# Attention followed by a three-way maxout FFN: the attention products regrouped, transposes moved to the DMA engines, and a new order of work

## The chip, the cores and the metric

The kernel runs on one core of one Trainium2 chip. The metric is the device time of one execution in microseconds (us); the kernel before takes 380.43 us as the median of 3 runs (380.34 to 380.91). The engines are called by the profile's names: PE is TensorE's matrix product and PEld its load of the stationary operand (the weights), DVE is VectorE, ACT is ScalarE, POOL is GpSimd, SP is SyncE. A matrix product streams the columns of its moving operand past a stationary operand of at most 128 rows by 128 columns and leaves float32 sums in PSUM, which has 8 banks of 512 float32 per partition.

## The reference, cut to what matters

```python
batch, n_heads, seq, head_dim = (8, 12, 448, 64)          # q, k, v: float32
n_tokens, d_model, d_ff = (3584, 768, 768)

def _attn_ref(q, k, v):
    scale = 1.0 / np.sqrt(q.shape[-1])
    scores = scale * np.matmul(q, k.transpose(0, 1, 3, 2))
    m = np.max(scores, axis=-1, keepdims=True)
    e = np.exp(scores - m)
    attn = e / (np.sum(e, axis=-1, keepdims=True) + np.exp(-m) + 1e-09)
    return np.matmul(attn, v)

def _moe_ref(x, w1, w2, w3, w_out):
    h = np.maximum(np.maximum(x @ w1, x @ w2), x @ w3)
    return h @ w_out

# x: the attention's output as (batch * seq, n_heads * head_dim)
```

Multiplying numerator and denominator by exp(m) gives exp(s) / (sum of exp(s) + 1), so both kernels take exp of the scaled scores without a maximum and add one to the sum.

## The kernel before

The 96 pairs of batch and head are worked in 24 groups of four heads, three groups to a batch. The 448 keys of a head lie in four chunks of 112. The loop interleaves the attention of a group with "pieces" of the FFN of an earlier batch: an up piece is six products of 448 columns into one bank (one of w1, w2, w3 and 128 of the 768 hidden features), an out piece six products of 384 columns. Parts that nothing below speaks of are cut.

```python
SC = 112; NCH = S // SC; GH = 4
ps1 = tile_pool("ps1", bufs=4, PSUM)      # one bank each: transposes, sums of AV, FFN pieces
ps2 = tile_pool("ps2", bufs=2, PSUM)      # two banks each: scores

def transpose_pair(i, pr):                # two heads: K and Q to [dim, token]
    for n, t16 in enumerate((k16, q16)):
        for c in range(NCH):
            nc.tensor.transpose(out=trT[:, n, ts(c, SC)], in_=t16[:, c, :, :], identity=...)
    nc.vector.tensor_copy(out=qkT, in_=trT...)

def scores_visit(i, pr, cs):              # two chunks of 112 keys for two heads
    for c in cs:
        for hh in range(2):
            nc.tensor.matmul(out=stp[:, hh, 0:S],
                lhsT=qkT[hh * D : hh * D + D, c * SC : c * SC + 128],
                rhs=qkT[hh * D : hh * D + D, S : 2 * S], start=True, stop=True)
    for c, stp in zip(cs, stps):
        nc.scalar.activation(out=eT[:, 2*pr : 2*pr+2, c, :], in_=stp[0:SC, :, 0:S],
                             func=AF.Exp, scale=scale)

def av_group(i):                          # sums over the keys, four heads side by side
    def col_tiled(weights):
        for c in range(NCH):
            for hh in range(GH):
                nc.tensor.matmul(out=bank[32*hh : 32*hh+32, 0:S], lhsT=weights(hh, c),
                                 rhs=eT[:, hh, c, :], ...)
    den = col_tiled(ones)                                   # sum of exp
    nc.scalar.activation(out=lnd, in_=den, func=AF.Ln, bias=one_b)
    nc.scalar.activation(out=rb, in_=lnd, func=AF.Exp, bias=ln_lam, scale=-1.0)
    for hf in range(2):
        num = col_tiled(v[:, hh, c, hf::2])                 # half of the 64 dims
        nc.vector.tensor_tensor(out=xT[...], in0=num, in1=rb, op=ALU.mult)

def up_piece(b, fc, i):
    for dc in range(NDC):                                   # 6
        nc.tensor.matmul(out=p_i[:, 0:S], lhsT=w_sb[i][:, dc, ts(fc, 128)],
                         rhs=xT[b][:, dc, :], ...)
    # DVE: copy (i == 0) or maximum with what is in hT

def out_piece(bp, t, nh):
    for fc in range(NFC):                                   # 6
        nc.tensor.matmul(out=op_ps[:, 0:384], lhsT=hT[bp][:, fc, ts(t, 128)],
                         rhs=wout_sb[:, fc, ts(nh, 384)], ...)
    # DVE: times 1/LAMBDA into o_sb; every second piece SP stores 128 rows

for i in range(24):                        # four visits for each group
    for vi, (pr, cs) in enumerate(visits):
        scores_visit(i, pr, cs)
        # vi == 0: FFN pieces, av_group(i - 1), FFN pieces, copies of K and Q by DVE
        # vi == 1, 2: FFN pieces, transpose_pair(i + 1, vi - 1), FFN pieces
        # vi == 3: FFN pieces
av_group(23); add_pieces(7); moe(all)
```

Of the kernel before, what the change touches and what calls it, by code (L numbers as in the profile page):

```python
# [14 lines left out]
ts = bass.ts  # L15

MMDT = FP16
LAMBDA = 256.0


@with_exitstack
def kernel(
# [16 lines left out]
    SC = 112  # L39
    NCH = S // SC  # L40
    NDC = DM // 128
    NFC = DFF // 128
    GH = 4
    NG = H // GH
    scale = 1.0 / math.sqrt(D)

    tabs = list(get_activation_tables(nc.m.arch).keys())
# [10 lines left out]
    cpool = ctx.enter_context(tc.tile_pool(name="const", bufs=1))  # L58
    ld_pool = ctx.enter_context(tc.tile_pool(name="ld", bufs=5))
    p16_pool = ctx.enter_context(tc.tile_pool(name="p16", bufs=2))  # L60
    att_pool = ctx.enter_context(tc.tile_pool(name="att", bufs=4))
    e_pool = ctx.enter_context(tc.tile_pool(name="e", bufs=2))
    small = ctx.enter_context(tc.tile_pool(name="small", bufs=2))
    xt_pool = ctx.enter_context(tc.tile_pool(name="xt", bufs=2))
    ht_pool = ctx.enter_context(tc.tile_pool(name="ht", bufs=2))
    out_pool = ctx.enter_context(tc.tile_pool(name="outp", bufs=3))

    ps1 = ctx.enter_context(tc.tile_pool(name="ps1", bufs=4, space=bass.MemoryType.PSUM))
    ps2 = ctx.enter_context(tc.tile_pool(name="ps2", bufs=2, space=bass.MemoryType.PSUM))

    ctx.enter_context(tc.manual_schedule())

    groups = [(b, g) for b in range(B) for g in range(NG)]
    raw = {}

    def load_group(i, which="qkv", step=GH):
        b, g = groups[i]
        tiles = raw.setdefault(i, {})
        for name in which:
            tiles[name] = ld_pool.tile(  # L80
                [SC, GH, NCH, D], MMDT, tag="ld_" + name, name="ld_" + name
            )
        for h0 in range(0, GH, step):
            for name in which:
                src = {"q": q, "k": k, "v": v}[name][b].rearrange(
                    "(g h) (p c) d -> g p h (c d)", g=NG, c=NCH
                )[g]
                nc.gpsimd.dma_start(  # L88
                    out=tiles[name][:, h0 : h0 + step].rearrange("p h c d -> p h (c d)"),
                    in_=src[:, h0 : h0 + step],  # L90
                )

    load_group(0, "qk", 2)
    ident16 = cpool.tile([128, 128], MMDT, name="ident16")
    make_identity(nc, ident16)
    load_group(1, "qk")
    load_group(0, "v")
    load_group(1, "v")
    load_group(2)
    ones16 = cpool.tile([SC, 32], MMDT, name="ones16")  # L100
    nc.vector.memset(ones16, 1.0)
    one_b = cpool.tile([128, 1], FP32, name="one_b")
    nc.vector.memset(one_b, 1.0)

    ln_lam = cpool.tile([128, 1], FP32, name="ln_lam")
    nc.vector.memset(ln_lam, math.log(LAMBDA))

    w_sb = [cpool.tile([128, NDC, DFF], MMDT, name=f"w{i}") for i in range(4)]
    wout_sb = w_sb[3]

    def load_weight(i):
        w = (moe_w1, moe_w2, moe_w3, moe_w_out)[i]
        for g in range(NG):
            if i < 3:
                src = w.rearrange("(g p hf) f -> g p hf f", g=NG, hf=2)[g]
            else:
                src = w.rearrange("(g hf p) f -> g p hf f", g=NG, hf=2)[g]
            nc.gpsimd.dma_start(out=w_sb[i][:, 2 * g : 2 * g + 2, :], in_=src)


    state = {}

    def pair_qk(i):
        qf, kf = raw[i].pop("q"), raw[i].pop("k")
        qk16 = []
        for pr in range(GH // 2):
            q16 = p16_pool.tile([SC, NCH, 2, D], MMDT, tag=f"q16_{pr}", name=f"q16_{pr}")
            k16 = p16_pool.tile([SC, NCH, 2, D], MMDT, tag=f"k16_{pr}", name=f"k16_{pr}")
            nc.vector.tensor_copy(
                out=k16, in_=kf[:, 2 * pr : 2 * pr + 2].rearrange("p h c d -> p c h d")  # L130
            )
            nc.vector.tensor_copy(
                out=q16, in_=qf[:, 2 * pr : 2 * pr + 2].rearrange("p h c d -> p c h d")
            )
            qk16.append((q16, k16))
        state[i] = {"qk16": qk16, "qkT": []}

    def transpose_pair(i, pr):
        st = state[i]
        q16, k16 = st["qk16"][pr]  # L140
        trT = ps1.tile([128, 2, S], MMDT, tag="bank1", name="trT")
        for n, t16 in enumerate((k16, q16)):
            for c in range(NCH):
                nc.tensor.transpose(  # L144
                    out=trT[:, n, ts(c, SC)], in_=t16[:, c, :, :],
                    identity=ident16[0:SC, 0:SC],
                )
        qkT = att_pool.tile([2 * D, 2 * S], MMDT, tag="qkT", name="qkT")
        nc.vector.tensor_copy(out=qkT, in_=trT.rearrange("p n s -> p (n s)"))  # L149
        st["qkT"].append(qkT)  # L150

    def scores_visit(i, pr, cs):
        st = state[i]
        if "eT" not in st:
            st["eT"] = e_pool.tile([SC, GH, NCH, S], MMDT, tag="eT", name="eT")
        qkT = st["qkT"][pr]
        stps = []
        for c in cs:
            stp = ps2.tile([128, 2, 512], FP32, tag="bank2", name="stp")
            for hh in range(2):  # L160
                nc.tensor.matmul(  # L161
                    out=stp[:, hh, 0:S],
                    lhsT=qkT[hh * D : hh * D + D, c * SC : c * SC + 128],
                    rhs=qkT[hh * D : hh * D + D, S : 2 * S],
                    start=True,
                    stop=True,
                )
            stps.append(stp)
        for c, stp in zip(cs, stps):
            nc.scalar.activation(  # L170
                out=st["eT"][:, 2 * pr : 2 * pr + 2, c, :],
                in_=stp[0:SC, :, 0:S],
                func=AF.Exp,
                scale=scale,
            )

    xT = {}

    def av_group(i):
        b, g = groups[i]  # L180
        st = state.pop(i)
        eT, v16 = st["eT"], raw[i].pop("v")
        if g == 0:
            xT[b] = xt_pool.tile([128, NDC, S], MMDT, tag="xT", name="xT")

        def col_tiled(weights):
            bank = ps1.tile([128, 512], FP32, tag="bank1", name="av")
            for c in range(NCH):
                for hh in range(GH):
                    nc.tensor.matmul(  # L190
                        out=bank[32 * hh : 32 * hh + 32, 0:S],
                        lhsT=weights(hh, c),
                        rhs=eT[:, hh, c, :],
                        start=(c == 0),
                        stop=(c == NCH - 1),
                    )
            return bank

        den = col_tiled(lambda hh, c: ones16[:, :])
        lnd = small.tile([128, S], FP32, tag="lnd", name="lnd")  # L200
        nc.scalar.activation(out=lnd, in_=den[:, 0:S], func=AF.Ln, bias=one_b)  # L201
        rb = small.tile([128, S], FP32, tag="rb", name="rb")
        nc.scalar.activation(out=rb, in_=lnd, func=AF.Exp, bias=ln_lam, scale=-1.0)  # L203
        for hf in range(2):
            num = col_tiled(lambda hh, c: v16[:, hh, c, hf::2])
            nc.vector.tensor_tensor(  # L206
                out=xT[b][:, 2 * g + hf, :], in0=num[:, 0:S], in1=rb, op=ALU.mult
            )

# [4 lines left out]
    def up_piece(b, fc, i):  # L214
        if b % 2 == 0 and fc == 0 and i == 0:
            hT[b // 2] = ht_pool.tile([128, NFC, 2 * S], MMDT, tag="hT", name="hT")
        dst = hT[b // 2][:, fc, (b % 2) * S : (b % 2) * S + S]
        p_i = ps1.tile([128, 512], FP32, tag="bank1", name="p_i")
        for dc in range(NDC):
            nc.tensor.matmul(  # L220
                out=p_i[:, 0:S],
                lhsT=w_sb[i][:, dc, ts(fc, 128)],
                rhs=xT[b][:, dc, :],
                start=(dc == 0),
                stop=(dc == NDC - 1),
            )
        if i == 0:
            nc.vector.tensor_copy(out=dst, in_=p_i[:, 0:S])  # L228
        else:
            nc.vector.tensor_tensor(out=dst, in0=dst, in1=p_i[:, 0:S], op=ALU.max)  # L230

    NH = 2
    NW = DM // NH

    def out_piece(bp, t, nh):
# [45 lines left out]
    def moe(cols):  # L281
# [5 lines left out]
        if not pieces:  # L287
            credit[0] = min(credit[0], 0.0)
# [82 lines left out]
```

## Time and profile before

| What | Value |
|---|---|
| time, median of 3 | 380.43 us |
| span in the profile | 377.6 us |
| PE busy | 358.3 us, 3120 products |
| DVE, ACT, POOL busy | 194.7, 194.5, 59.4 us |
| read from and written to HBM | 42.47 MB, 11.01 MB |
| first FFN product | 39.22 us after the start of the span |
| last FFN product of the last piece | ends at about 373 us |

The profile gives each engine's busy time, the span in 40 slices, the chain of work that ended last, and groups of like instructions with the mean duration of one. Two things are needed to read it. A product's duration (353 ns for 448 columns) is its latency, from the first column in to the last sum out; products in a row overlap, so what a product costs is the distance from its start to the next start. Where the timeline merges a row of x like products that last t us together and d us each, that distance is (t - d) / (x - 1). And the share of a busy engine is an average over a start, a long middle and an end, which have different limits; the stretches of time show them apart.

### The profile page before, as it was taken

To read this page: it belongs to the slowest core of one execution; us is meant where nothing else is said; L and a number is where in the kernel's file an instruction comes from. 1 tells how busy PE (TensorE), PEld (TensorE's weight loads), DVE (VectorE), ACT (ScalarE), POOL (GpSimd) and SP (SyncE) were. 2 spreads that over 40 slices of the span, in tenths; PEclk is the share of its full clock that TensorE was granted. 3 is DMA by queue.
4 is the path that set the end of the run, shared out by engine and by line. 5 is a ranking of instruction groups with operands and counts; after the bars stand their busy time and mean duration, and the time that the engine had idled before them with its cause. 6 is when DMAs were issued, how large, how long until landed. Compare 5 with 4: busy or idle time off the path is not lost.

```text
span 377.6 us, 7320 instructions
## 1 busy us (share of the span) xinstructions
PE 358.3 (95%) x3120; PEld 172.0 (46%) x3120; DVE 194.7 (52%) x395; ACT 194.5 (52%) x241; POOL 59.4 (16%) x92
## 2 busy tenths in 40 slices
PE   2777999999999999999999999999999999999995
PEld 1233444544445444454445544454444554445552
DVE  2233545545546546546546555455465465445553
ACT  1879464663655655555555645546555554552000
POOL 8533450220210201202202202202000000000000
PEclk9999999999999999999999999999999999999999
DMA  7999998555508625455236555077010410013005
GB/s 92 185 208 206 204 196 121 73 136 68 73 2 151 111 54 75 60 139 75 32 43 89 126 101 73 6 128 141 2 26 0 128 43 0 2 32 95 2 0 168
DMA packets 40064, 32.71 MB, mean 87 GB/s; under 512 B 2272, under 2 KB 35296, under 8 KB 40032
## 3 DMA queue, kind: packets, MB, share of 16 engines
q0 software_dynamic: 35552, 21.24, 40.8%
q1 hardware_dynamic: 4480, 11.01, 9.8%
q8 instruction: 24, 0.39, 0.5%
q14 instruction: 8, 0.07, 0.0%
HBM read 42.47 MB, written 11.01 MB: 142 GB/s over the span
## 4 chain that ended last, share of the span: by engine, by line
PE 84%; DMA 9%; ACT 2%; POOL 2%; DVE 1%; issue 1%; DVEq 0%; POOLq 0%
PE p_i L220 43%; PE op_ps L241 15%; PE av L190 11%; PE stp L161 10%; PE trT L144 4%; DMA w_123<-in_moe_w_dram 3%; DMA ld_k<-in_k_dram 3%; DMA ld_q<-in_q_dram 2%; DVE xT L206 1%; ACT eT L170 1%; ACT rb L203 1%; ACT lnd L201 1%; POOL ld_q L88 1%; POOL ld_k L88 1%; POOL ld_v L88 0%
## 5 line engine op out<-in xcount | busy, mean ns | idle before, releaser
L170 ACT ACTIVATE eT<-stp 112x896 f16<-112x896 f32 x192 | 164.9, 916 | 145.1 <-PE stp L161 145.1
L230 DVE TENSOR_TENSOR hT<-hT,p_i 128x448 f16<-128x448 f16 x96 | 59.4, 619 | 45.5 <-PE p_i L220 45.1
L206 DVE TENSOR_TENSOR xT<-av,rb 128x448 f16<-128x448 f32 x48 | 27.8, 619 | 70.8 <-ACT rb L203 64.7
L220 PE MATMUL p_i<-xT,w_122 128*128 128x448 f16 x288 | 63.0, 353 | 0.4
L220 PE MATMUL p_i<-xT,w_123 128*128 128x448 f16 x288 | 62.4, 353 | 0.0
L220 PE MATMUL p_i<-xT,w_124 128*128 128x448 f16 x288 | 62.2, 353 | 0.0
L161 PE MATMUL stp<-qkT 64*128 64x448 f16 x384 | 56.3, 364 | 4.9 <-ACT eT L170 4.8
L241 PE MATMUL op_ps<-w_125,hT 128*128 128x384 f16 x336 | 59.5, 326 | 0.0
L88 POOL DMA_DIRECT2D ld_v<-in_v_dram x24 | 16.8, 702 | 192.3 <-PE av L190 126.3
L248 DVE TENSOR_SCALAR o_sb<-op_ps 128x384 f32<-128x384 f32 x56 | 31.2, 557 | 28.5 <-PE op_ps L241 28.4
L241 PEld LDWEIGHTS <-hT 128*128 128x128 f16 x336 | 30.9, 98 | 24.8 <-issue 6.3
L190 PE MATMUL av<-eT,ld_v 112*32 112x448 f16 x768 | 41.8, 361 | 0.0
L228 DVE CAST hT<-p_i 128x448 f16<-128x448 f32 x48 | 29.7, 620 | 19.9 <-PE p_i L220 19.9
L220 PEld LDWEIGHTS <-w_123 128*128 128x128 f16 x288 | 25.9, 98 | 29.6 <-issue 9.2
L220 PEld LDWEIGHTS <-w_124 128*128 128x128 f16 x288 | 26.0, 98 | 28.7 <-issue 7.8
L220 PEld LDWEIGHTS <-w_122 128*128 128x128 f16 x288 | 26.1, 98 | 27.8 <-issue 7.0
L149 DVE COPY qkT<-trT 128x896 f16<-128x896 f16 x48 | 29.5, 615 | 3.1 <-PE trT L144 3.0
L161 PEld LDWEIGHTS <-qkT 64*128 64x128 f16 x384 | 12.0, 94 | 40.9 <-issue 40.3
L190 PEld LDWEIGHTS <-ld_v 112*32 112x32 f16 x768 | 21.0, 99 | 16.8 <-issue 1.7
L190 PE MATMUL av<-eT,ones_116 112*32 112x448 f16 x384 | 23.3, 364 | 0.0
L88 POOL DMA_DIRECT2D ld_q<-in_q_dram x25 | 17.7, 709 | 6.9 <-DMA w_124<-in_moe_w_dram 1.5
L88 POOL DMA_DIRECT2D ld_k<-in_k_dram x25 | 17.6, 703 | 4.4 <-DMA w_123<-in_moe_w_dram 1.1
(305 smaller groups left out, 142.1 us busy)
## 6 DMA issues: line engine op xcount, KB each, us to landing
ld_v<-in_v_dram POOLq DMA_DIRECT2D x24, 224.0 KB, 4.0
ld_q<-in_q_dram POOLq DMA_DIRECT2D x23, 224.0 KB, 4.9
ld_k<-in_k_dram POOLq DMA_DIRECT2D x23, 224.0 KB, 5.9
out_dram<-o_sb SPq DMA_DIRECT2D x8, 336.0 KB, 2.8
out_dram<-o_sb SPq DMA_DIRECT2D x8, 288.0 KB, 2.7
out_dram<-o_sb SPq DMA_DIRECT2D x8, 240.0 KB, 2.8
out_dram<-o_sb SPq DMA_DIRECT2D x8, 192.0 KB, 2.7
w_122<-in_moe_w_dram POOLq DMA_DIRECT2D x3, 384.0 KB, 10.7
```

The lines of the kernel that those rows point to most:

```text
L88: nc.gpsimd.dma_start(out=tiles[name][:, h0 : h0 + step].rearrange("p h c d -> p h (c d)"), in_=src[:, h0 : h0 + step],)
L144: nc.tensor.transpose(out=trT[:, n, ts(c, SC)], in_=t16[:, c, :, :], identity=ident16[0:SC, 0:SC],)
L149: nc.vector.tensor_copy(out=qkT, in_=trT.rearrange("p n s -> p (n s)"))
L161: nc.tensor.matmul(out=stp[:, hh, 0:S], lhsT=qkT[hh * D : hh * D + D, c * SC : c * SC + 128], rhs=qkT[hh * D : hh * D + D, S : 2 * S], sta ...
L170: nc.scalar.activation(out=st["eT"][:, 2 * pr : 2 * pr + 2, c, :], in_=stp[0:SC, :, 0:S], func=AF.Exp, scale=scale,)
L190: nc.tensor.matmul(out=bank[32 * hh : 32 * hh + 32, 0:S], lhsT=weights(hh, c), rhs=eT[:, hh, c, :], start=(c == 0), stop=(c == NCH - 1),)
L206: nc.vector.tensor_tensor(out=xT[b][:, 2 * g + hf, :], in0=num[:, 0:S], in1=rb, op=ALU.mult)
L220: nc.tensor.matmul(out=p_i[:, 0:S], lhsT=w_sb[i][:, dc, ts(fc, 128)], rhs=xT[b][:, dc, :], start=(dc == 0), stop=(dc == NDC - 1),)
L228: nc.vector.tensor_copy(out=dst, in_=p_i[:, 0:S])
L230: nc.vector.tensor_tensor(out=dst, in0=dst, in1=p_i[:, 0:S], op=ALU.max)
L241: nc.tensor.matmul(out=op_ps[:, 0:NW], lhsT=hT[bp][:, fc, ts(t, 128)], rhs=wout_sb[:, fc, ts(nh, NW)], start=(fc == 0), stop=(fc == NFC - 1),)
L248: nc.vector.tensor_scalar(out=o_sb[:, ts(nh, NW)], in0=op_ps[:, 0:NW], scalar1=1.0 / LAMBDA, scalar2=None, op0=ALU.mult,)
```

## The change

The kernel keeps its arithmetic (float16 operands, float32 sums, exp without a maximum) and its FFN pieces. Almost everything around them is new:

- **Tokens in blocks of 64.** A head's 448 tokens are seven blocks of 64. The scores of a block pair are four products of 64 rows by 64 columns ("quadrants" of the array), one unit of four quadrants filling two banks; a group has seven units in place of eight of the old pairs of products.
- **The sums over the keys are turned round.** The exps are the stationary operand and V, with a column of 1/LAMBDA behind it, is the moving one: 65 columns a product. The denominator comes out in column 65, so the products with ones and the Ln and Exp of ACT go; DVE adds 1/LAMBDA and takes a reciprocal. The result has tokens on partitions and has to be transposed for the FFN.
- **Transposes by DMA.** From group 7 on K and Q, and from group 6 on x, are transposed by DMA instructions of SP; earlier groups use PE. A half of the transposed Q is copied to the other partitions by POOL.
- **Seven visits for three groups.** From group 6 on, a visit holds three units of scores and the sums of one pair of heads, mixed quadrant by quadrant, then FFN pieces.
- **One-bank sums.** The seven sums of a pair in such a visit (three query windows of two heads and a shared remainder) lie in one bank; an instruction of ACT that does nothing orders the two halves.
- **A different start.** The first pair of heads is loaded in float32 by the queues of SP and ACT, and copied to float16; PE runs products of zeros meanwhile. Groups 0 to 2 are worked first for the odd-numbered parts of the queries (192 of 448), then for the rest, and the FFN of batch 0 starts on the first part.
- **The end.** The last row of output is stored in smaller parts on two queues, and the last batch's first product goes to the bank that is free.
- **PSUM.** Three slots of two banks and two single banks, handed out by hand, in place of four single and two double buffers.

The diff's core, with cuts marked by `...`:

```diff
-    SC = 112
-    NCH = S // SC
+    HP = 64
+    T = S // HP
+    D1 = D + 1
-    ps1 = ctx.enter_context(tc.tile_pool(name="ps1", bufs=4, space=bass.MemoryType.PSUM))
-    ps2 = ctx.enter_context(tc.tile_pool(name="ps2", bufs=2, space=bass.MemoryType.PSUM))
+    slots = [ps.tile([128, 2, 512], FP32, name=f"ps{j}") for j in range(3)]
+    banks = [ps.tile([128, 512], FP32, name=f"pb{j}") for j in range(2)]
+    for nm, src, eng in (("k", k, nc.sync), ("q", q, nc.scalar)):
+        first[nm] = cpool.tile([P, T, D], FP32, name="first_" + nm)
...
+    def transpose_dma(i):
...
+        for dst, nm, o in ((QT[i], "q", 4), (KT[i], "k", 0)):
+            nc.sync.dma_start_transpose(
+                out=dst[:, o * 128 : (o + T) * 128].rearrange("p (j x) -> p j x", x=P),
+                in_=raw[i][nm][:, 1 : NB + 1].rearrange("x t d -> x (t d)"),
+            )
...
+    def visit(units, pair):
+            def score(par, half, i=i, u=u, stp=stp):
...
+                return nc.tensor.matmul(
+                    out=stp[half * HP : half * HP + HP, par, 0:S],
+                    lhsT=k_block(i, pr, h2, x[half]),
+                    rhs=q_cols(i, pr, h2, par, "EO"), ...
+        def small_tiles(r, c, start):      # 64 rows x 64 columns x 65: 7 on a diagonal quadrant, 6 off it
...
+        def wides():                       # 128 x 128 x 65
+            for hh in range(2):
+                for j in range(3):
+                    for c, x in enumerate((X1, X3, X2)):
+                        nc.tensor.matmul(
+                            out=ps[:, (3 * hh + j) * D1 : (3 * hh + j + 1) * D1],
+                            lhsT=eF[:, o : o + 128],
+                            rhs=vx[:, 2 * pr + hh, (x[0]), 0:D1], ...
+        if qk:
+            (s0, _), (s1, _), (s2, _) = qk
+            for at in anti:
+                s0(*at)
+            turned = turn_over(smalls(diag, True))
+            for s, at in ((s0, diag), (s1, anti), (s1, diag), (s2, anti), (s2, diag)):
+                for corner in at:
+                    s(*corner)
+            smalls(anti, False, turned)
+            for _, power in qk:
+                power()
+            wides()
...
+    for g in range(ONE, NI, 3):
+        todo = [(g + n // 7, n % 7) for n in range(21)]
+        for n in range(7):
+            us = todo[3 * n : 3 * n + 3]
+            plan.append(...)
...
+    turn["b"] = 0
+    fill(float("inf"))
+    add_batch(B - 1)
+    fill(float("inf"))
```

The instruction lists of the two programs, counted by kind:

| PE products | before | after |
|---|---|---|
| FFN up, 448 columns (or 256 and 192) | 864 | 756 (and 108 and 108) |
| FFN out, 384 columns (or 256 and 128) | 336 | 330 (and 6 and 6) |
| scores | 384 of 448, 64 rows x 128 | 588 of 448, 84 of 256, 84 of 192, 64 x 64 |
| sums over keys | 1152 of 448, 112 x 32 | 924 of 65, 128 x 128, and 1148 of 65, 64 x 64 |
| transposes | 384 of 112 | 170 of 128 |
| products of zeros | 0 | 12 of 512 |
| changes between a full array, parts of 64 and parts of 32 | 200 | 140 |

ACT has 192 exps of 896 elements and 24 pairs of Ln and Exp before, and 147 exps of 896 with 24 of 384 to 1024 after. SP has 52 DMA transposes after and none before.

## The prediction

> **What bounds the kernel now.** I read the page's table of busy time and its 40 slices first. Of each slice row the digits are tenths of busy time; each of the 40 digits is 9.4 us.
>
> ```profile
> PE 358.3 (95%) x3120; PEld 172.0 (46%) x3120; DVE 194.7 (52%) x395; ACT 194.5 (52%) x241; POOL 59.4 (16%) x92
> PE   2777999999999999999999999999999999999995
> PEclk9999999999999999999999999999999999999999
> DMA  7999998555508625455236555077010410013005
> ```
>
> From slice 5 on PE is never free, at full clock; DVE and ACT are half idle. In the first four slices PE has gaps while the DMA engines are full. So there are two stages, and I ask of each what PE does in it. Next the sums over stretches of time; columns are the stretch, its length, and busy us of PE, PEld, DVE, ACT, POOL, then clock, DMA share, GB/s.
>
> ```profile
> 20.00:30.00 10.00, 7.91 (x108) 3.42 (x100) 3.30 (x8) 8.16 (x12) 3.73 (x6) 1.00 1.17 207
> 118.00:162.00 44.00, 44.00 (x393) 21.23 (x392) 24.54 (x51) 24.20 (x30) 6.29 (x9) 1.00 0.50 84
> 373.50:377.60 4.10, 0.00 (x0) 0.00 (x0) 0.01 (x1) 0.00 (x0) 0.00 (x0) 0.91 0.40 127
> ```
>
> One batch (three groups) costs 44 us, all of it PE. The early stretch has the loads at 207 GB/s and ACT at 82%. After PE's last product 4.1 us go to the last copy and store. A busy PE is not yet a cost per product, so I read PE's timeline in the middle, one visit:
>
> ```profile
> 180.55 1.30 PE L220 MATMUL p_i<-xT,w_123 128*128 128x448 f16 x6
> 181.78 0.55 PE L161 MATMUL stp<-qkT 64*128 64x448 f16 x4
> 182.26 0.94 PE L190 MATMUL av<-eT,ones_116 112*32 112x448 f16 x16
> 183.03 1.69 PE L190 MATMUL av<-eT,ld_v 112*32 112x448 f16 x32
> 184.65 1.31 PE L220 MATMUL p_i<-xT,w_124 128*128 128x448 f16 x6
> ...
> 187.52 0.36 PE L144 MATMUL trT<-ident_97,k_0_2523 112*128 112x112 f16 x4
> 187.72 0.36 PE L144 MATMUL trT<-ident_97,q_0_2522 112*128 112x112 f16 x4
> 187.91 0.35 PE L220 MATMUL p_i<-xT,w_123 128*128 128x448 f16 x1
> ```
>
> A product of 448 columns lasts 0.353 us as latency, so its slot is (1.30 - 0.353) / 5 = 0.189 us. Eight transposes of 112 columns start in 187.91 - 187.52 = 0.39 us, 0.049 each. The line through both is 0.417 ns a column and 2.3 ns fixed. Scores with 64 rows go two to a slot, sums with 32 columns four to a slot (12 slots of 0.189 between 182.26 and 184.53). And there is a gap at each change of shape: the six up products end their slots at 180.55 + 6 x 0.189 = 181.69, the scores start at 181.78; two slots later it is 182.16, the sums start at 182.26; those end at 184.53, the next starts at 184.65. That is 0.09 to 0.12 us, 0.093 as the mean.
>
> **What the skill says.** The Trainium skill, "TensorE: Matmul & The Clock Gate", section "Back-to-back issue gap", gives N / 2.4 + 2.5 ns for an isolated product; my line agrees. The same section also states about 81 ns for 128-column products with their own weight load in a stream; here 112 columns take 49, so I go by the measurement. "TensorEngine Tiling (Array Packing)", section "Key Properties", says that a change of tiling mode drains the engine; the 0.093 us agrees. The first page's section on fast weight load says that a 128-column load of a type other than float32 is read four chunks at a time. The two rows below fit: the last number of the first pair is the mean duration, 98 ns for 128 columns and 99 for 32. No trace here shows products shorter than 112 columns, which the change lives on.
>
> ```profile
> L220 PEld LDWEIGHTS <-w_123 128*128 128x128 f16 x288 | 25.9, 98 | 29.6 <-issue 9.2
> L190 PEld LDWEIGHTS <-ld_v 112*32 112x32 f16 x768 | 21.0, 99 | 16.8 <-issue 1.7
> ```
>
> "DMA: Bandwidth & Descriptors", section "DMA Transpose (X-bar)", allows transposes of 2-byte types from SP. No run here shows one.
>
> **PE's ledger before, in slots.** Up 864 x 0.189 = 163.5; out 336 x 0.1625 = 54.6; scores 384 / 2 x 0.189 = 36.3; sums 1152 / 4 x 0.189 = 54.5; transposes 384 x 0.049 = 18.8; 200 changes of shape x 0.093 = 18.6. Sum 346.3 us. As a test: the first FFN product starts at 39.22, with about 16 us of the ledger behind it (three groups of scores and sums at 3.8, four of transposes at 0.8, some changes). The other 330 should fill 39.2 to 373.5, which is 334. So 1.2% is missing from the ledger, and the start wastes 39 - 16 = 23 us.
>
> **The change, part by part, on the same scale.**
> - FFN: the same columns. Up 756 x 0.189 + 108 x 0.109 + 108 x 0.082 = 163.6; out 54.6. Change 0.
> - Scores: quadrants, four at a time if they run side by side as the pairs did: 588 / 4 x 0.189 + 84 / 4 x (0.109 + 0.082) = 31.8. Saves 4.5, the eighth that padded 112 to 128.
> - Sums over keys: 924 full products of 65 columns at 65 x 0.417 + 2.3 = 29.4 ns give 27.2. 1148 quadrant products, two at a time, give 574 x 0.0294 = 16.9. In the 37 visits with scores and a pair, seven double steps stand beside the first two score quadrants and six beside the last: 7 x 0.029 + 3 x 0.189 = 0.77 us in place of 3 x 0.189 + 13 x 0.029 = 0.95, so 6.5 less. 37.6 in all against 54.5: saves 16.9.
> - Transposes: 170 x 0.0557 = 9.5 against 18.8: saves 9.3, if the DMA ones arrive in time. The DMA engines are at half share or below after 118 us, so there is room.
> - Changes of shape: 140 x 0.093 = 13.0 against 18.6: saves 5.6. This is what seven visits for three groups in place of twelve buys.
> - Products of zeros: 12 x 0.216 = 2.6 more, in the waiting start.
>
> Sum after 312.7, that is 33.6 less. A middle batch is 20.4 up, 6.8 out, 4.0 scores, 4.2 sums, 1.3 changes: 36.7 us against 44.
>
> **The start.** PE's work ahead of the first FFN product is about 14 us by the list of instructions (zeros, transposes, scores, sums, changes). That product needs the first weight matrix. Its three loads were issued at 9.5 to 12.1 us and took a median 10.7 us, so it was there near 21 to 23; the same bytes stand ahead of it now, and I take 20.5. So 6.5 us of waiting. The second matrix comes after 5.4 MB in all; at 207 GB/s that is 26 us, with 3 of start 29, and PE gets there at about 28. ACT has by then some 20 us of exps and copies after a first one at 5, so it is about as late. I take 9 us of waste in place of 23: saves 14.
>
> **The end.** Smaller last stores: 3.5 us in place of 4.1. **ACT and DVE** lose work: ACT 48 Ln and Exp (31 us) and 45 exps of 0.916, and gains some copies; DVE loses the copies of K, Q and transposed K, Q, and gains about 1 us for each of 48 pairs. Both stay near 180 of 330. They bind nowhere but in the start.
>
> **Sum.** 312.7 + 1.2% (3.8) + 9 + 3.5 = 329. The device time was 380.43 for a span of 377.6, so add 2.8: **332 us**.
>
> **The rivals.** First, short products don't reach 29 ns: the load or the issue of each binds at, say, the 49 ns of the transposes. For: nothing here shows less; 4324 products with a load each in place of 3120. Against: the load overlaps, and in a switch four loads and four products start within 15 ns. It would cost 924 x 19.6 = 18 us and up to 11 for the quadrants: 350 to 360. Second, PSUM turnaround becomes the wait: two single banks and three slots, shared by scores, sums and FFN pieces, with DVE's 0.62 us copies now behind the four small DVE steps of each pair. For: one bank holds all sums of a pair and must be read before the next pair. Against: DVE is half idle, and a visit is 5 us long. At 0.3 us in each of 44 visits it makes 345. Third, transfers: DMA transposes share SP's queue with the stores and could arrive late, or the start is as bound to the loads as before. Late transposes would show as PE waits in each visit; a start unchanged at 23 us gives 346. Fourth, all of it lies off the path: excluded, since PE's slots are the path from 39 us on.
>
> **Range and chances.** Each rival alone ends below 360, well under 380. The ledger's fixed part (FFN, 218 us) is certain; the uncertain terms are the sums (37.6, could be 30 to 55), the start (9, could be 5 to 18) and waits (3.8, could be 2 to 12). That makes 322 to 347 for 8 in 10. Faster by over 2% 0.97, within 2% 0.02, slower 0.01.
>
> **What would show each step.** Full 65-column products starting 29 to 31 ns apart prove the sums; 45 or more is rival one. Quadrant scores four to a 0.19 us slot, and a visit's part before the full products near 0.77 us, prove the mixing. About 0.09 us at each change of shape. The first FFN product near 20 us. PE at 9 in nearly all slices after the third; a wait of PE on DVE or ACT in each visit is rival two, on a DMA transpose rival three. A middle batch above 40 us, or a first FFN product after 30 us, makes the prediction wrong.

## The result and the profile after

The changed kernel takes 337.93 us as the median of 4 runs (337.11 to 338.33), the kernel before on the same chip 380.38. The ratio is 0.889 with a 95% interval of 0.8866 to 0.8915. The prediction was 332 with a range of 322 to 347. The span in the profile is 335.3 us for 377.6 before.

Page of the changed kernel, busy time and slices (each digit is 8.4 us):

```profile
PE 324.7 (97%) x4324; PEld 201.1 (60%) x4324; DVE 202.9 (60%) x489; ACT 149.9 (45%) x181; POOL 146.4 (44%) x260
PE   7899899999999999999999999999999999999993
PEclk9999999999999999999999999999999999999999
DMA  8999999899998969899899989999899711133016
```

PE is at 9 from the third slice on, but for an 8 in the fifth. The DMA row has changed most: before, most slices from the eighth on were at 6 or below, and now all but one are at 8 or 9 until slice 31. Two stretches of the changed kernel, with the same columns as in the prediction:

```profile
200.00:240.00 40.00, 40.00 (x559) 23.69 (x558) 24.50 (x57) 18.58 (x23) 23.05 (x41) 1.00 1.07 148
332.00:335.30 3.30, 0.00 (x0) 0.00 (x0) 0.00 (x0) 0.00 (x0) 0.00 (x0) 1.00 0.28 86
```

In the middle PE has no idle time, as before, and the DMA share is 1.07 where it was 0.50.

PE's timeline of one visit in the middle. Columns: start, length of the merged row, line and operation, tiles, rows x columns of the array used, shape, count:

```profile
201.12 0.73 PE L594 MATMUL pb<-xT,w 128*128 128x448 f16 x3
201.78 0.38 PE L414 MATMUL ps<-QT,KT 64*64 64x448 f16 x2
201.79 0.31 PE L452 MATMUL pb<-vt,e 64*64 64x65 f16 x8
201.93 0.23 PE L452 MATMUL pb<-vx,e 64*64 64x65 f16 x4
201.99 0.35 PE L414 MATMUL ps<-QT,KT 64*64 64x448 f16 x2
...
202.41 0.35 PE L414 MATMUL ps<-QT,KT 64*64 64x448 f16 x2
202.43 0.23 PE L452 MATMUL pb<-vt,e 64*64 64x65 f16 x4
202.50 0.26 PE L452 MATMUL pb<-vx,e 64*64 64x65 f16 x6
202.70 0.73 PE L481 MATMUL pb<-vx,e 128*128 128x65 f16 x18
203.27 0.35 PE L594 MATMUL pb<-xT,w 128*128 128x448 f16 x1
```

The last up product's slot ends at 201.12 + 3 x 0.189 = 201.69. Scores and small sums stand side by side from 201.78, the eighteen full products follow at 202.70, the next up product at 203.27. From the end of one FFN slot to the next FFN start that is 1.58 us. The start times of all 37 such visits give a median of 1.586, which I use below; the five visits with scores alone take 0.787. The full products are (0.73 - 0.194) / 17 = 31.5 ns apart here; the mean of all 646 distances is 31.9.

**Where the 42.3 us of span went.** The first FFN product starts at 22.23 us instead of 39.22: 17.0 less. From there to the end of the last product's slot it is 307.7 instead of 333.5: 25.8 less. From there to the end of the span it is 5.35 instead of 4.87: 0.5 more. The seven middle visits of a batch have a mean period of 37.9 us, the batch before 43.9.

### The profile page after: what moved, and what is told of

Same layout as the page of the kernel before. It is cut to its first block, busy times and chain, and to the rows that moved or that the text cites. A ratio compares the mean times of both kernels' runs of the same rounds, so it can differ in the third digit from the quotient of the medians.

```text
span 335.3 us, 10275 instructions
## 1 busy us (share of the span) xinstructions
PE 324.7 (97%) x4324; PEld 201.1 (60%) x4324; DVE 202.9 (60%) x489; ACT 149.9 (45%) x181; POOL 146.4 (44%) x260
## 4 chain that ended last, share of the span: by engine, by line
PE 92%; ACT 3%; DVE 2%; issue 1%; ACTq 0%; DVEq 0%
PE pb L594 32%; PE ps L594 15%; PE pb L618 9%; PE ps L618 8%; PE ps L414 8%; PE pb L481 7%; PE pb L452 4%; PE ps L322 3%; PE ps L379 2%; ACT e L342 2%; PE pb L195 1%; DVE QT L210 1%; PE ps L362 1%; ACT QT L208 1%; PE pb L247 1%
## 5 line engine op out<-in xcount | busy, mean ns | idle before, releaser
L425 ACT ACTIVATE e<-ps 128x896 f16<-128x896 f32 x126 | 106.5, 917 | 120.9 <-PE ps L414 99.1
L594 PEld LDWEIGHTS <-w 128*128 128x128 f16 x972 | 90.7, 98 | 65.7 <-issue 1.4
L594 PE MATMUL pb<-xT,w 128*128 128x448 f16 (+2 forms) x690 | 124.5, 324 | 0.3 <-ACT QT L208 0.2
L267 POOL COPY QT<-QT 64x384 f16<-64x384 f16 (+1 forms) x84 | 46.7, 556 | 97.4 <-DMA QT<-ld_q 64.3
L594 PE MATMUL ps<-xT,w 128*128 128x448 f16 (+1 forms) x282 | 57.8, 349 | 0.0
L605 DVE TENSOR_TENSOR hT<-hT,pb 128x448 f16<-128x448 f16 (+2 forms) x59 | 36.6, 620 | 19.0 <-PE pb L594 15.3
L342 ACT ACTIVATE e<-ps 128x896 f16<-128x896 f32 (+4 forms) x45 | 36.4, 869 | 15.6 <-PE ps L322 15.3
L414 PE MATMUL ps<-QT,KT 64*64 64x448 f16 x504 | 40.4, 354 | 0.0
L618 PE MATMUL pb<-w,hT 128*128 128x384 f16 (+2 forms) x180 | 32.6, 321 | 0.2 <-DVE hT L605 0.2
L618 PE MATMUL ps<-w,hT 128*128 128x384 f16 x162 | 28.4, 326 | 0.0
```

The costliest lines, as they stand in the source:

```text
L267: eng.tensor_copy(out=t[d0 : d0 + HP, o * 128 : (o + n) * 128], in_=t[s0 : s0 + HP, a * 128 : (a + n) * 128],)
L342: nc.scalar.activation(out=dst, in_=src, func=AF.Exp, scale=scale)
L414: return nc.tensor.matmul(out=stp[half * HP : half * HP + HP, par, 0:S], lhsT=k_block(i, pr, h2, x[half]), rhs=q_cols(i, pr, h2, par, "EO" ...
L425: nc.scalar.activation(out=dst, in_=stp[:, :, 0:S], func=AF.Exp, scale=scale)
L594: nc.tensor.matmul(out=p_i[:, j * qn : (j + 1) * qn], lhsT=w_sb[i][:, dc, ts(fc, 128)], rhs=xT[b][:, dc, q0 : q0 + qn], start=(dc == 0), s ...
L605: nc.vector.tensor_tensor(out=dst, in0=dst, in1=src, op=ALU.max)
```

## The experiments

Each of them is a change to the changed kernel, except the first and the last. "Visit" is the median from FFN slot end to FFN start, from the start times in the trace.

### The slots by themselves

A kernel with PE products on constant data and nothing else; its output is zeros.

```diff
+    full(5, 65, 120)      # 128 x 128 x 65, own weight load each, 120 in a row; likewise 128 ... 16
+    quads(4, 65, 60, diag)  # 64 x 64 x 65, two quadrants at a time
```

> A kernel of products alone, on constant data, that writes zeros as its output: 120 full products each of 128, 112, 96, 80, 65, 64, 48, 32 and 16 columns in a row, each with its own 128-column weight load, and 60 double steps of 64-by-64 quadrants with 65 columns. My line (0.417 ns a column and 2.3 fixed) expects 55.7, 49, 42, 35.7, 29.4, 29, 22, 15.6 and 9 ns from start to start. The changed kernel showed 31.9 at 65. If the load of the weights or the issue of instructions is a floor, the row flattens below some count: a floor at 30 to 32 would make 65, 48, 32 and 16 all alike. If instead only the data of the changed kernel slow it (sums into the same columns, odd widths), 65 comes out at 29.4 here. For the double step: 29.4 if two quadrants run side by side with their loads hidden, near 32 as the changed kernel showed, 59 if they go one after the other. Changes of shape near 0.09 us.

Three stretches of its PE timeline, and one with the quadrants:

```profile
18.81 2.38 PE L51 MATMUL bk<-mv,we 128*128 128x112 f16 x45
33.82 2.35 PE L51 MATMUL bk<-mv,we 128*128 128x65 f16 x72
40.83 2.33 PE L51 MATMUL bk<-mv,we 128*128 128x48 f16 x87
...
57.32 1.66 PE L62 MATMUL bk<-mv,we 64*64 64x65 f16 x94
```

With durations of 213, 193 and 183 ns, (2.38 - 0.213) / 44 = 49 ns, (2.35 - 0.193) / 71 = 30.4 and (2.33 - 0.183) / 86 = 25.0. All of the row, from the start times:

| columns | 128 | 112 | 96 | 80 | 65 | 64 | 48 | 32 | 16 |
|---|---|---|---|---|---|---|---|---|---|
| ns from start to start | 55.8 | 49.2 | 42.5 | 35.8 | 30.4 | 29.2 | 25.0 | 25.0 | 25.0 in the second half |

The line of the prediction holds down to 64 columns; at 48 and fewer the distance stays at 25.0 ns. At 65 columns most distances are 29 and about each fifth is 35, which 64 columns don't show. The double step of the quadrants takes 31.7 ns after a first one of 52, so two quadrants do run side by side. Of the 31.9 ns in the changed kernel 30.4 come with the width; what adds the last 1.5 there wasn't tried.

### The small sums not mixed with scores

```diff
-            for at in anti:
-                s0(*at)
             turned = turn_over(smalls(diag, True))
-            for s, at in ((s0, diag), (s1, anti), (s1, diag), (s2, anti), (s2, diag)):
+            for s, at in ((s0, anti), (s0, diag), (s1, anti), (s1, diag), (s2, anti), (s2, diag)):
```

> The changed kernel, but in each of the 37 visits with both, the small sums of the diagonal quadrants come ahead of all scores and those of the other two behind them, so that they do not stand beside scores. Theory (quadrants run side by side): a visit's part before the full products grows from 0.917 us to about 0.095 + 13 x 0.031 + 3 x 0.19 = 1.06, so 37 x 0.15 = 5.4 us: 343. Rival (quadrants do not overlap across kinds, mixing buys nothing, the gain came from elsewhere): 338 within 0.5.

340.64 us (340.12 to 341.69), 2.7 more. A visit takes 1.673: 0.087 more, and 37 x 0.087 = 3.2. Half of the expected size. The start times show why: though the first scores stand behind the small sums in the program, they start while those still run, 0.09 us before the last of them. So part of the mixing comes about by itself, on quadrants that are free; the written order gets the rest.

### Two more changes of shape in each visit

```diff
-            for s, at in ((s0, diag), (s1, anti), (s1, diag), (s2, anti), (s2, diag)):
+            for s, at in ((s0, diag), (s1, anti), (s1, diag)):
...
             smalls(anti, False, turned)
-            wides()
+            wides((0,))
+            for corner in anti + diag:
+                s2(*corner)
+            wides((1,))
```

> The changed kernel with the same products, but the third unit's scores stand between the two heads' full products, so that each of the 37 visits has two more changes of shape. Theory (each change drains PE and PE's slots are the path): 37 x 2 x 0.093 to 0.125 = 7 to 9 us more: 345 to 347. Rival (the drain hides behind waits for DVE, ACT or transposes that are as long): under 3 us more.

352.11 us (351.80 to 352.76), 14.2 more: too much for the theory. A visit takes 1.995, 0.409 more. The edit also moved the second half of the small sums ahead of the third unit, so the next run makes that move alone.

### The second half of the small sums earlier, no more changes

```diff
             for s, at in ((s0, diag), (s1, anti), (s1, diag)):
...
             smalls(anti, False, turned)
+            for corner in anti + diag:
+                s2(*corner)
```

> The changed kernel with the second half of the small sums ahead of the third unit's scores instead of behind them; no more changes of shape. It tells apart why two more changes of shape in each visit cost 14 us and not 7 to 9 (in that run this order was used too, and there the small sums waited about 0.15 us for ACT's instruction that does nothing). Theory (the wait on that instruction comes out from behind the scores): 37 x 0.13 to 0.16 = 5 to 6 us more, 343 to 344, which leaves 8 for 74 changes, 0.11 each. Rival (the changes of shape themselves cost 0.19 each): 338 to 339.5.

343.94 us (343.65 to 344.52), 6.0 more. A visit takes 1.772, 0.186 more, and 37 x 0.186 = 6.9. Of this kernel's waits, in us in total, times, and the longest:

```profile
PEld L452 <- ACTq L472: 8.4, 36, 0.2
```

36 visits wait 0.2 us for ACT's instruction that does nothing; the changed kernel's list of waits has no such line. So the wait is there to be had, and the order as written hides it behind the third unit. What is left for the two changes is 1.995 - 1.772 = 0.223 us, 0.112 each, or in time (352.11 - 343.94) / 74 = 0.110. The drain of the prediction is confirmed as time on the path, at 0.11 in place of 0.093.

### Nine visits for three groups

```diff
-    for g in range(ONE, NI, 3):
-        todo = [(g + n // 7, n % 7) for n in range(21)]
...
+    for i in range(ONE, NI):
+        for vi, us in enumerate(((0, 1), (2, 3), (4, 5, 6))):
+            plan.append(([(i, us)], (i - 1, vi) if vi < 2 else None))
...
-    adds = {NV0 + 3: 1, **{NV0 + 7 * (b - 1) + 2: b for b in range(2, B - 1)}}
+    adds = {NV0 + 3: 1, **{NV0 + 9 * (b - 1) + 2: b for b in range(2, B - 1)}}
```

> The changed kernel with three visits for each group (nine for three groups, two, two and three units) from group 6 on, in place of seven with three units each; 168 changes of shape in place of 140, the same products. Theory (a visit costs its two changes of shape): 28 x 0.093 to 0.125 = 2.6 to 3.5 us more: 340.5 to 341.5. Rival (what counts is how well small sums and scores mix, and two units in a visit mix as well): 338 within 0.5. A third way: shorter stretches between visits leave DVE or ACT less time, and it costs over 5.

376.06 us (373.37 to 378.23), 38 more, far beyond all three. Its waits of PE and of its weight load:

```profile
PE pb L594 <- DMA xT<-xn: 17.4, 5, 5.3
...
PEld L452 <- ACTq L472: 7.7, 36, 0.2
```

Three things add up. First, my plan let the FFN of a new batch begin in the very next visit after that batch's last pair; the seven-visit plan has a visit without sums in between, and the DMA transpose of x lands meanwhile. At the first of the five waits SP issues that transpose at 118.38, behind six stores in its queue; PE is ready at 120.06 and starts at 123.58. In all 17.4 us. Second, visits: 36 with two units take 1.582, 18 with three units and no sums 0.788, against 37 of 1.586 and 5 of 0.788 after: with the last pairs, 1.41 each, 74.0 us instead of 64.0, 10 more. The 28 changes are 3 of it; the rest is that a pair's visit costs the same with two units as with three, since a wait of 0.2 us for ACT stands where the third unit was. Third, in four stretches near these waits, 23.9 us together, the granted clock is 0.50; PE is busy for 17.6 of them, which makes about 9 us lost (an estimate: half of the busy time). That is 36 of the 39.6 us between the two spans. The run can't give the cost of changes alone, and it isn't a fair nine-visit kernel; one with a later start of each batch's FFN wasn't tried.

### DMA transposes of K and Q twice

```diff
-        for dst, nm, o in ((QT[i], "q", 4), (KT[i], "k", 0)):
+        for dst, nm, o in 2 * ((QT[i], "q", 4), (KT[i], "k", 0)):
```

> The changed kernel with each DMA transpose of K and Q issued twice in a row (34 more). Theory (the transposes lie beside PE's work with slack): 338 within 1. Rival (the DMA engines are near full in the middle, share 1.0 where the kernel before had 0.5, so another 30 per cent delays loads and transposes until PE waits): 345 or more.

360.86 us (356.37 to 365.43), 23 more. Two of the four runs, 363.15 and 365.43, count as slow, and the trace is of the first of them; the other two, 356.37 and 358.56, are 18.4 and 20.6 more. That is the rival's number, but not for its reason. The largest of PE's waits (us in total, times, longest), then SP's issues ahead of the longest one (start, length of the issue):

```profile
PE pb L594 <- DMA xT<-xn: 18.8, 5, 7.2
```

```profile
150.94 1.23 SPq L259 DMA_TRANSPOSE QT<-ld_q  x1
152.27 1.25 SPq L259 DMA_TRANSPOSE KT<-ld_k  x1
155.25 1.22 SPq L259 DMA_TRANSPOSE QT<-ld_q  x1
159.36 1.22 SPq L259 DMA_TRANSPOSE KT<-ld_k  x1
160.64 1.30 SPq L577 DMA_TRANSPOSE xT<-xn  x1
```

The second transpose of Q writes the tile of the first, and SP waits until the first has landed before it issues the second; so with K. In the trace these are 26 waits of SP's queue, 65.4 us in all, and the changed kernel has none of them. The transpose of x stands behind them and is issued at 160.64; PE is ready from 156.60 on and starts at 163.81. Once issued, a transpose of x lands sooner here than in the changed kernel (count, median us to landing; here, then there):

```profile
xT<-xn SPq DMA_TRANSPOSE x18, 3.5
```

```profile
xT<-xn SPq DMA_TRANSPOSE x18, 4.5
```

Those of Q take 5.7 against 5.9, and those of K 5.6 against 6.1. So what PE waits for is a late issue in SP's queue, and not DMA engines that are too full; how much room these have left, the run doesn't show. The granted clock falls to 0.50 at 160.0 us, 3.4 us into the wait, and is 1.00 again at 166.8, so the first 3.0 us of work after the wait run at half clock, and the wait costs more than its length. In the changed kernel no wait of PE on a DMA is listed: there the transposes are hidden.

### The first products without the first matrix

```diff
-                    lhsT=w_sb[i][:, dc, ts(fc, 128)],
+                    lhsT=wz[:, 0:128] if (b, i, q0) == (0, 0, NE) else w_sb[i][:, dc, ts(fc, 128)],
```

It leaves out the first matrix for a part of batch 0, so the output there is not the reference's.

> The changed kernel with the first three up pieces (first matrix, odd part of batch 0) multiplying by a tile of zeros that is there from the start instead of the first weight matrix, whose loads stay. Theory of my prediction (the first FFN product waits for the first matrix): it starts earlier than 22.2 us, by up to 2 us, and the end comes earlier by about as much. Rival (the chain of the critical path: scores, exps, sums and copies of groups 0 to 2 set it; the matrix was there before): first FFN product at 22.2 within 0.2, time 338 within 0.4.

338.37 us (337.24 to 339.69). First FFN product of this kernel, then of the changed one:

```profile
22.67 1.29 PE L594 MATMUL pb<-xT,wz 128*128 128x192 f16 x12
```

```profile
22.23 1.29 PE L594 MATMUL pb<-xT,w 128*128 128x192 f16 x12
```

Without any wait for weights it starts no earlier; 22.67 is outside the rival's 0.2, but in the traces of the other runs that keep this start it lies between 22.2 and 23.2. In the changed kernel the three loads of the first matrix landed at 17.88, 19.81 and 21.64, the last of them 0.6 us ahead of that product. What does set it is the chain just before; columns are start, length, what:

```profile
16.82 0.81 ACT e L342
17.67 0.26 PE ps L362 x8
17.93 0.48 PE ps L379 x12
18.41 0.37 PE ps L322 x8
...
20.83 0.24 PE pb L554 x4
21.09 0.16 DVE rb L389
21.28 0.19 DVE rb L392
21.49 0.43 DVE xn L395
21.98 0.28 PE pb L554 x2
22.26 1.27 PE pb L594 x12
```

Exps, sums, reciprocal and transposes follow one another on PE, ACT and DVE, with no DMA among them. The first FFN product comes as early as the attention of groups 0 to 2 lets it.

### No products of zeros; first loads by POOL

```diff
-    warm(8)
-    warm(4)
```

> The changed kernel without its twelve products of zeros (3.4 us before the first real product and 1.0 us at 8.35). Theory (they stand in waiting time and only bring PE to full clock before the transposes, which cost 107 ns apiece instead of 56 while it is cold): the first 49 transposes and 56 score quadrants cost twice, of which part hides behind ACT: 1 to 2.5 us more, about 339.5. Rival (they only take PE's time): 338 to 337, up to 1 us less.

```diff
-        eng.dma_start(out=first[nm].rearrange("x t d -> x (t d)"), in_=pair)
...
+    load_qk(0, "kq", (0, 1))
...
-    evac(DV, raw[0]["k"][:, 1 : T + 1], first["k"])
-    evac(AC, raw[0]["q"][:, 1 : T + 1], first["q"])
```

> The changed kernel with the first pair of heads loaded by POOL's queue with the cast, like all others, and without the two copies from float32. Now: issued at 0.74 on two queues, landed at about 4.0, copied by 4.5. By POOL: issued at 1.25, then 1.9, landing 3.4 to 3.8 us later, so at 5.3 to 5.7, and every later load on that queue 1.4 us later. Theory (the start is a chain that begins with this load): 1 to 2 us more, about 339.5. Rival (the start waits for later data, the weights above all, which come 1.4 us later at most and share the same engines): 338.5 or less.

339.47 us (338.44 to 340.22) without zeros, 338.83 (338.31 to 339.17) with POOL's loads. The ratio to the kernel before is 0.8941 (0.8918 to 0.8964) without zeros, just clear of the changed kernel's interval (0.8866 to 0.8915), so this run is slower by a little; with POOL's loads it is 0.8922 (0.8900 to 0.8944), which overlaps it, so that is not established as time. The traces say more. First transposes without zeros, and in the changed kernel:

```profile
4.69 0.50 PE L231 MATMUL ps<-ident,ld_k 128*128 128x128 f16 x3 [4.69 <-DVE ld_k L210]
```

```profile
4.54 0.34 PE L231 MATMUL ps<-ident,ld_k 128*128 128x128 f16 x3
```

Unwarmed, they are slower, and the first FFN product comes at 24.16 us; with POOL's loads at 24.12. Both are later than any of the other traces, 22.2 to 23.2, and fit a start that is one chain from the first load on. Of the 1.9 us in these two traces about 1.5 and 0.9 are left in the medians.

### One last store for each half row

```diff
-                cuts = [(0, NW, None), (NW, 256, (sy, sc)), (NW + 256, 128, (sy, sc))]
+                cuts = [(0, NW, None), (NW, 256, None), (NW + 256, 128, (sy, sc))]
```

> The changed kernel with the last row's cuts of products kept (384, 256 and 128 columns) but one store for each half of the row at the end, on the two queues, in place of two stores for each half. Theory (after the last product the end is one issue of 0.7 us behind another on each queue, and then a landing of 3.1 to 3.5 us that hardly depends on the size): 0.5 to 0.7 us less, 337.3. Rival (the landing grows with 192 KB in place of 32): the same or up to 0.5 more.

337.55 us (336.97 to 337.81): 0.4 less, within the spread of both, so not established. ACT's part of the end in the changed kernel, then here (start, length of the issue, count):

```profile
330.15 1.39 ACTq L635 DMA_DIRECT2D out_dram<-o_sb  x2
```

```profile
330.57 0.55 ACTq L635 DMA_DIRECT2D out_dram<-o_sb  x1
```

The last issue ends 0.4 us earlier. The landing is 3.5 us at 192 KB here and 3.5 at 32 KB after, so cutting the store doesn't shorten it. No run here beats the changed kernel by more than the spread.

### The free bank not first

```diff
-    turn["b"] = 0
```

> The changed kernel without the line that gives the last pieces the free bank first. Theory (the last batch's pieces alternate between two banks and the first one then waits for the bank that DVE still reads): one DVE step of 0.56 to 0.62 us with its signals, 0.3 to 0.9 us more: 338.5. Rival: nothing that can be measured.

338.49 us (338.20 to 338.98), 0.6 more; the intervals again overlap. The trace has the expected wait, and the changed kernel has none there:

```profile
302.39 1.86 PE L594 MATMUL pb<-xT,w 128*128 128x448 f16 x9 [0.65 <-DVE o_sb L625]
```

### The kernel before without its products with ones

```diff
-        den = col_tiled(lambda hh, c: ones16[:, :])
...
-        nc.scalar.activation(out=lnd, in_=den[:, 0:S], func=AF.Ln, bias=one_b)
+        lnd = lnd_c
```

The denominator is a constant, so the output is not the attention's.

> The kernel before with the products with ones and the Ln left out (the factor is taken from a constant, so the output is not the attention's). Theory (PE's slots are its path, everything else lies beside them): 24 groups x 4 slots x 0.189 = 18.2 us less: 362. Rival (a good part of the attention's products lay beside other limits, the loads in the first 40 us above all): the three groups of the start give nothing, 16 us less at most: 364 to 366; if ACT's chain was the limit in each visit, far more than 18.

363.54 us (363.00 to 363.82), 16.6 less. In the middle the period of a group falls from 14.52 to 13.79 us, 0.73, nearly the four slots of 0.189 (0.757). The first FFN product comes 2.2 earlier, so the start's sums were on the path too, against the rival. But the sum is 1.6 short of 18.2. Between the first FFN product and the next group's sums 1.4 us are given back: PE waits there 1.72 us for DVE's copy of K, where it waited 0.32 before. The granted clock, 0.74 from 24 to 37 us where it was 1.00 before, may have cost some of the gain ahead of that; this isn't shown. PE's slots are the path in the middle; in the start they are only part of it.

## Why the prediction was right, and where it was off

The time lies in the range and the mechanism is the predicted one: PE's slots are the path from the first FFN product on, and the change removes slots. The median is 6 us above the point. By the prediction's own steps:

- **FFN, the same columns.** Right: 0.189 and 0.163 us a product, as before.
- **Sums over the keys, 37.6 us.** Right in kind, too small in size. The full products are 31.9 ns apart and not 29.4; the double steps about 32, with a first one of 53. The part of a visit with quadrants is 0.92 us with one drain of 0.095, so 0.82, and not 0.77. A visit takes 1.586 us in place of 0.093 + 0.773 + 0.093 + 0.529 = 1.488: 37 x 0.098 = 3.6 us, the largest single miss. The 240 full products of the start add 0.7. Of the 6.5 us that I gave to the mixing, the run with the sums apart loses 2.7; about half comes without the written order.
- **Changes of shape.** Right: 0.094 into the quadrants, 0.11 by experiment. What "seven visits" buys was counted too low: the changes are only part of it, the third unit rides along in a visit of the same length (1.586 with three, 1.582 with two).
- **Transposes.** 9.5 us of PE stay (170 slots of 0.056), the others are hidden. But "so there is room" was not a statement of slack: it read the share before the change, an average (slices 27 and 28 of its row show 7), and after the change it is 1.07 in place of 0.50. That is no ceiling either: between 158 and 160 us of the doubled run it is 1.74. What made transposes late in the doubled run was their place in SP's queue, which the prediction's third rival names first. How much room is left stays open.
- **The start.** "That product needs the first weight matrix": this step failed. 22.2 us against 20.5 is near by luck: the matrix was complete at 21.6, and it is the chain of attention that sets the start, as the run without the matrix shows. Gap less work fell from 39.2 - 16 to 22.2 - 14, so by 15.0 where 14 was predicted.
- **The end.** 3.5 us in place of 4.1 predicted, 0.6 less. From the end of the last product's slot it is 5.35 in place of 4.87, 0.5 more (the prediction's 4.1 began at 373.5, about 0.8 later than this measure). Smaller stores add issues and don't land sooner.
- **ACT and DVE near 180.** Wrong for both: 149.9 and 202.9. DVE gained 21 us of small steps that copy 64 x 64 remainders (76 of 280 ns). Off the path, so without effect.
- **The rivals.** Short products at 49 ns: refuted by the slots alone. PSUM turnaround: no wait of PE for a bank in the middle; it shows as soon as the order is disturbed, 0.65 us in the last bank, 0.2 in each visit behind ACT. Late transfers: not in this kernel; they appear when SP issues the transposes of x late, as 18.8 and 17.4 us of waits in two of the runs.

The misses by term are 3.6 for visits, 0.7 for early sums, 1.7 for the start and 1.9 for the end: 7.9. The span was 6.3 over the predicted 329.0; the 1.6 between them is what the allowance for waits (3.8) gave back, as a remainder and not as a measurement.

How the 42.3 us divide among the parts of the change is the ledger's account. No run takes back the DMA transposes, the turned sums or the split of the first queries alone, so the worth of each is argued and not measured.

## What to carry to other kernels

Where one engine has no idle time, count its slots from start to start and its drains, not its busy time. Here that gave the time of a large rewrite within 2%, and the saving as 48 us where 42 were measured. When work is moved to another engine, look at the order in its queue as well as at its share: here a transpose that stood behind others, or behind stores, turned into waits of up to 7 us and a halved clock, while its own landing was no slower. Filling a visit until its waits are covered was worth more here than the drains that it saves.

## What the runs showed of the hardware that was not expected

Full products with their own 128-column weight load go down to 25.0 ns from start to start, at 48 columns and fewer; 65 columns cost 30.4 ns, 64 cost 29.2. Scores on free quadrants start up to 0.09 us ahead of small sums that stand before them in the program. A DMA transpose holds the engines about twice as long per byte as a store, as an estimate from the time that the packets took: the 34 added transposes moved 7.80 MB and brought SP's queue from 41.0% of the 16 engines' span of 335.3 us to 52.0% of 361.4 us, 6.5 us for a MB; before, the stores took 9.8% of 377.6 us for 11.0 MB, 3.4 us for a MB. And in a wait of PE of 7.2 us the granted clock fell to 0.50 after 3.4 us, and was full again only 3.0 us after the work went on.
